# Norm outputs in chunks of 96 columns with ones behind each chunk: diagonal sums and plain sums from the same matmuls, in the backward pass of a spectral block with a gated MLP

## The chip, the cores and the metric

The kernel runs on one core of a Trainium2 chip. A core has five engines with queues of their own: TensorE (PE, with PEld for its weight loads), VectorE (DVE), ScalarE (ACT), GpSimd (POOL) and SyncE (SP, here used to issue DMAs). Engines run their instructions in order and wait for one another through semaphores. The metric is the device time of one execution, in microseconds (us).

## The reference

One block with two modulated norms, a global spectral filter (A) and a gated bilinear MLP (B), and then the gradients of the whole by its eight inputs. S = 2048 rows, D = 576 columns, F = 4608, everything in bfloat16.

```python
mod = (silu(c) @ w_mod)                     # six rows of 576: sa, ca, ga, sb, cb, gb
h = layernorm(x) * (1 + ca) + sa
x = x + ga * irfft2(rfft2(h) * (w_r + 1j * w_i))
h = layernorm(x) * (1 + cb) + sb
x = x + gb * ((h @ w_gate) * (h @ w_up)) @ w_down
out, vjp = jax.vjp(f, x, w_r, w_i, w_gate, w_up, w_down, c, w_mod)
grads = vjp(grad_out)
```

The change is about the gradients of the modulation rows. With gh the gradient at h (one row of 576 for each of the 2048 positions) and n the norm's output, the gradient of a shift row (sa, sb) is the plain sum of gh over the positions, and that of a scale row (ca, cb) is the sum of gh · n over the positions, column by column. ga's row is the sum of gx · y in the same way (gx the gradient, y the filter's output); gb's is made earlier.

## The kernel before

Positions are worked in 16 tiles of 128 (NT = 16), the columns of the MLP in blocks of 128 (NFB = 36). A forward part makes the two norms and the spectral filter, a long middle part (on PE nearly throughout) makes the gradients of the MLP, and a tail (from L811) makes the backward of the second norm, of the spectral filter and of the first norm. Into the tail's stages the MLP's last projection is woven, so that PE always has work.

What the change touches:

- **Norm outputs.** The stage of the first norm (L359 to L383) makes n1 on ACT (L372) from x, in groups of 4 tiles, uses it on DVE (nm, L374) and stores it to DRAM (n1_d, L378, on POOL). The stage of the second norm (L554 to L578) does the same for n2 in groups of 2 tiles (L570, L572, L575). The tiles come from pools that rotate two buffers.
- **Tail stage 1**, backward of the second norm: a pipeline of four steps over the 16 tiles (t1_norm L969, t1_turn L995, t1_cols, t1_rows). t1_norm loads n2's and y's tile, multiplies (gn) and calls norm_back (L868). t1_turn makes a transpose and adds the tile's part of the modulation sums into three PSUM banks csA, csB, csC.
- **Tail stage 2** (L1131 to L1178): the spectral filter's backward, untouched by the change.
- **Tail stage 3**, backward of the first norm: t3_rows L1194, t3_cols L1202 and t3_norm L1216 over 16 tiles, with the sums in csD and csE. t3_cols builds gh on DVE from two PSUM banks, one of them copied by ACT (ye, L1212; gh's halves L1213 and L1214). t3_norm makes gn (L1223) and calls norm_back, whose steps for the first norm are: ACT u with its row sum (L871), DVE product with its row sum (L873), DVE ab (L875), DVE u + residual (L876), ACT w (L878), DVE ob (L881). `ld3["last"]` is the last of these.
- **The sums.** PE has no sum of elementwise products, so `diag` (L910) multiplies gh (as weights) by n, 128 columns by 128 columns, over the positions; the wanted sums stand on the diagonal of each 128 x 128 product, and all tiles add up in the same bank. Four chunks of 128 columns and one of the last 64 make 576. `colsum` (L907) makes the plain sums: pick, a matrix of zeros with 64 columns of ones, as weights, and half of gh (288 columns) as the moving side, one matmul for each half, into rows 0 to 63 and 64 to 127 of one bank. The banks are opened and closed by matmuls of zeros (add_zero, L902).
- **Getting the sums out.** `diag_rows` (L917) masks the diagonals with the identity on DVE (dcb, dga, dca). The plain sums are copied (dsb L1043, dsa L1240). Each is spread to all 128 partitions by a matmul (`spread`, L924): of_rows (L930) with a matrix of ones, of_sums (L933) with sel, two masks that POOL fills at L1104.
- **Sections.** `section` (L936) takes one row of sums, copies the two spread halves into dmb on ACT (L939; dmb has two buffers), loads the slice of w_mod, multiplies on ACT (o8) and on DVE (pr, L952, five products with sums). Six sections hang on tiles of the last projection loop (L1264 to L1305): MSB at tile 8, MCB 9, MGA 10, MGB 11, MSA 12, MCA 13, each traced under an order constraint behind the tile's last matmul and behind ld3["last"].
- **What sets the order.** A scheduler orders each engine's instructions by priority and readiness in its own time. On PE `deal` (L883) writes the order of the tail's steps out by hand and deals a fixed number of projection matmuls into each step (16 a step in stage 1, 12 in stage 2, 20 and then 16 in stage 3); the spreads are not in that list and are placed by the scheduler.

Of the kernel before, what the change touches and what calls it, by code (L numbers as in the profile page):

```python
# [9 lines left out]
FP32 = mybir.dt.float32  # L10
# [9 lines left out]
NT = 16  # L20
S = 2048
D = 576
DP = 640
DF = 289
FP = 292
# [73 lines left out]
def build(ctx, tc, A_x, A_w_r, A_w_i, B_w_gate, B_w_up, B_w_down, c_in, w_mod, grad_out,  # L99
# [13 lines left out]
    def dram(name, shape, dt):  # L113
        return nc.dram_tensor(name, list(shape), dt).ap()
# [10 lines left out]
    wn_d = dram("wn_d", [128, 2 * NT * FP], BF)  # L125
    n1_d = dram("n1_d", [128, NT, D], BF)
    n2_d = dram("n2_d", [128, NT, D], BF)
    MSA, MCA, MGA, MSB, MCB, MGB = range(6)
# [12 lines left out]

    pick = glob.tile([128, 2, 128], BF, name="pick")
    nc.vector.memset(pick[:], 0.0)
    for q in range(2):
        nc.vector.memset(pick[:, q, 64 * q:64 * q + 64], 1.0)


    def traced():
# [111 lines left out]
    with ExitStack() as hs:  # L260
# [98 lines left out]
        def s1_norm(t):  # L359
            c4, tt = t // 4, t % 4  # L360
            if tt == 0:
                if c4 == 1:
                    with tc.issue_after(first):
                        x_load(3)
                n1s[c4] = hw2.tile([128, 4, D], BF, name="n1")
            if t == 0 or tt == (1 if c4 == 0 else 0):
                n = 1 if t == 0 else 4 - tt
                nmr = norm_stats(xts[c4][:, tt:tt + n, :], hw2, n, "ln1", rstd1g[:, t:t + n], 4)
                for k in range(n):
                    n1s["nmr", t + k] = nmr[:, k:k + 1]  # L370
# [3 lines left out]
            nc.vector.tensor_tensor(out=nm[:], in0=n1[:, tt, :], in1=modh[MCA][:], op=MUL)  # L374
# [157 lines left out]


        uts, ybs, h2_made = {}, {}, []

# [18 lines left out]
        def s3_norm(sa):  # L554
# [14 lines left out]
            for i in range(2):  # L569
                nc.scalar.activation(out=n2[:, i, :], in_=x1[:, i, :], func=ACT.Identity, bias=nmr2[:, i:i + 1], scale=rstd2g[:, s0 + i:s0 + i + 1])  # L570
                nm = hw2.tile([128, D], BF, name="nm")
                nc.vector.tensor_tensor(out=nm[:], in0=n2[:, i, :], in1=modh[MCB][:], op=MUL)  # L572
                nc.vector.tensor_tensor(out=h2p[:, s0 + i, D:DP], in0=nm[:, 512:D], in1=modh[MSB][:, 512:D], op=ADD)
                h2_made.append(nc.vector.tensor_tensor(out=h2p[:, s0 + i, 0:D], in0=nm[:], in1=modh[MSB][:], op=ADD).ins)
# [236 lines left out]
    with ExitStack() as ts:  # L811
# [56 lines left out]
        def norm_back(pool, gn, n, rstd, res, out, name):  # L868
# [6 lines left out]
            nc.vector.tensor_scalar(out=ab[:], in0=s12[:], scalar1=-1.0 / D, scalar2=None, op0=MUL)  # L875
            nc.vector.tensor_tensor(out=u[:], in0=u[:], in1=res, op=ADD)  # L876
            if name == "1":
                nc.scalar.activation(out=w[:], in_=n, func=ACT.Identity, bias=ab[:, 0:1], scale=ab[:, 1:2])  # L878
            else:
                nc.vector.tensor_scalar(out=w[:], in0=n, scalar1=ab[:, 1:2], scalar2=ab[:, 0:1], op0=MUL, op1=ADD)  # L880
            return nc.vector.tensor_tensor(out=out, in0=u[:], in1=w[:], op=ADD)  # L881
# [19 lines left out]

        def add_zero(*banks, first):  # L902

            for cs in banks:
                nc.tensor.matmul(cs[:], lhsT=ident[:], rhs=zero[:], start=first, stop=not first)

        def colsum(cs, h, src):  # L907
            nc.tensor.matmul(cs[:, 0:288], lhsT=pick[:, h, :], rhs=src, start=False, stop=False)

        def diag(cs, cs4, off, a, b):  # L910

            for m in range(5):
                o = cs[:, wide(m)] if m < 4 else cs4[:, off:off + 64]
                w = 128 if m < 4 else 64
                nc.tensor.matmul(o, lhsT=a[:, wide(m)] if m < 4 else a[:, D - 128:D], rhs=b[:, m * 128:m * 128 + w], start=False, stop=False)

        def diag_rows(pool, cs, cs4, off, name):  # L917

            d = pool.tile([128, D], FP32, name=name)
            nc.vector.tensor_tensor(out=d[:, 0:512].rearrange("p (m n) -> p m n", m=4), in0=cs[:].rearrange("p (m n) -> p m n", m=4), in1=ident[:].unsqueeze(1).to_broadcast([128, 4, 128]), op=MUL)  # L920
            nc.vector.tensor_tensor(out=d[:, 512:576], in0=cs4[:, off:off + 64], in1=ident[:, 64:128], op=MUL)
            return d
# [10 lines left out]
        def of_sums(d):  # L933
            return [lambda h=h: spread(sel[:, h, :], d[:]) for h in range(2)]

# [18 lines left out]
        with ExitStack() as r1:  # L954
# [14 lines left out]
            def t1_norm(t):  # L969
                if t == 0:  # L970
                    nc.sync.dma_start(ga_h[:], modb_d[:, MGA, :])
                for k, src, tt in [("n2c", n2_d, 0)] * (t == 0) + [("n2c", n2_d, t + 1)] * (t < NT - 1) + [("yc", y_d, t)]:
                    ld[k, tt] = c1.tile([128, D], BF, name=k, bufs=5 if k == "n2c" else 3)
# [21 lines left out]
            def t1_turn(t):  # L995
# [7 lines left out]
                if t == 0:  # L1003
                    add_zero(csA, csB, csC, first=True)
# [34 lines left out]
            in_order(seq)  # L1039
            dcb = diag_rows(tl, csA, csB, 288, "dcb")  # L1040
            dga = diag_rows(tl, csC, csB, 352, "dga")
            dsb = tl.tile([128, 288], FP32, name="dsb")
            nc.vector.tensor_copy(dsb[:], csB[:, 0:288])  # L1043
            with behind([i_ for i_ in nc.cur_bb.bb.instructions[-40:] if i_.engine == mybir.EngineType.DVE][-1:]):
# [57 lines left out]
        with behind([last[nc.gpsimd]]):  # L1102
            gb_h = modh(MGB, "gb_h", gbhp, nc.gpsimd)
            for q in range(2):  # L1104
                nc.gpsimd.tensor_copy(sel[:, q, :], ident[:, 64 * q:64 * q + 1].to_broadcast([128, 128]))
            nc.gpsimd.memset(ones_b[:], 1.0)
            nc.gpsimd.memset(gsc[:], 0.0)
# [108 lines left out]
        def t3_norm(sa):  # L1216
            for k, src in (("n1c", n1_d), ("gxc", gx1_d)):
                ld3[k] = c3.tile([128, D], BF, name=k, bufs=5)
                nc.sync.dma_start(ld3[k][:], src[:, sa, :])
# [7 lines left out]
            if sa == 0:  # L1227
                add_zero(csD, csE, first=True)
# [9 lines left out]
        dca = diag_rows(tl, csD, csE, 288, "dca")  # L1238
# [141 lines left out]
```

## Time and profile before

| | us |
|---|---|
| runs of the kernel, median of 3 (lowest to highest) | 1526.43 (1525.81 to 1529.65) |
| the profiled execution, its own time | 1524.87 |
| its span in the trace | 1523.1 |
| tail stage 1 | about 1260 to 1335 |
| tail stage 2 | about 1335 to 1390 |
| tail stage 3 | about 1390 to 1454 |
| the rest, projection and sections | 1454 to the end |

In the rows of a timeline the first number is the start in us from the span's start, the second the duration, then engine, line, operation, output and inputs, their sizes, and how many instructions in a row the entry holds; a bracket gives the idle time of the engine ahead of it and what ended that. In groups the last numbers are busy time and mean ns, then idle time before. A duration of one matmul holds the length of its pipeline; a stream of them overlaps. "clock" in a window's row is the granted TensorE clock as a share of full speed.

### The profile page before, as it was taken

How to read it: one execution, taken by the hardware profiler on the slowest of the kernel's cores; microseconds unless marked ns; L12 is line 12 of the kernel's file. 1: busy time of each engine (PE TensorE's matmuls, PEld its weight loads, DVE VectorE, ACT ScalarE, POOL GpSimd, SP SyncE). 2: the span in 40 equal slices, each digit the busy share in tenths (PEclk: the TensorE clock that was granted, in tenths of full speed). 3: DMA queues.
4: the chain of work that ended last, by engine and by line, in shares of the span. 5: the costliest groups of instructions: out<-in, count | busy, mean ns of one | idle time of the engine just before them, and what ended most of it. 6: DMA issues, size and time to landing. Idle time of an engine off the chain costs nothing. (4 is left out here: it accounts for less than half of the span.)

```text
span 1523.1 us, 29031 instructions
## 1 busy us (share of the span) xinstructions
PE 1490.3 (98%) x11140; PEld 1012.6 (66%) x11144; DVE 1060.6 (70%) x2646; ACT 583.4 (38%) x1189; POOL 238.8 (16%) x363
## 2 busy tenths in 40 slices
PE   6899999999999999999999999999999999999998
PEld 4666543566666667666666676676666667888876
DVE  6866753666677767667677677676676768688884
ACT  6667742322222222222222222222222225686763
POOL 0001222101101102111111120120110113221022
PEclk9999999999999999999999999999999999999999
DMA  8968999688878768768778588688677779965587
GB/s 317 282 200 224 278 255 249 152 162 155 174 129 161 155 125 174 152 125 177 135 146 178 118 159 164 119 163 156 137 152 153 132 175 252 305 220 181 182 290 201
DMA packets 487181, 280.42 MB, mean 184 GB/s; under 512 B 408865, under 2 KB 457378, under 8 KB 486018
## 3 DMA queue, kind: packets, MB, share of 16 engines
q1 hardware_dynamic: 458882, 175.32, 55.6%
q0 software_dynamic: 28160, 103.25, 23.0%
q8 instruction: 87, 1.43, 0.4%
q14 instruction: 52, 0.43, 0.1%
HBM read 108.62 MB, written 82.31 MB: 125 GB/s over the span
## 5 line engine op out<-in xcount | busy, mean ns | idle before, releaser
L752 DVE TENSOR_TENSOR acc<-acc,u8p 128x288 f32<-128x288 f32 (+1 forms) x1088 | 483.3, 453 | 276.1 <-PE u8p L747 272.6
L747 PE MATMUL u8p<-wT,ggT 128*128 128x288 bf16 x1152 | 328.0, 286 | 1.7 <-DVE acc L752 1.6
L747 PE MATMUL u8p<-wT,guT 128*128 128x288 bf16 x1152 | 327.6, 286 | 0.0
L711 PE MATMUL gup<-h2T,wgu 128*128 128x512 bf16 x1152 | 297.8, 379 | 0.0
L646 ACT CAST so<-u57p 128x288 bf16<-128x288 f32 x216 | 86.3, 400 | 532.8 <-PE u57p L644 522.1
L644 PE MATMUL u57p<-h2p,gu_sf 128*128 128x288 bf16 x1152 | 186.4, 286 | 0.0
L644 PE MATMUL u57p<-h2p,gg_sf 128*128 128x288 bf16 x1152 | 185.9, 286 | 0.0
L711 PEld LDWEIGHTS <-wgu 128*128 128x128 bf16 x1152 | 109.6, 98 | 97.9 <-issue 17.1
L747 PEld LDWEIGHTS <-ggT 128*128 128x128 bf16 x1152 | 112.6, 98 | 66.5 <-issue 14.0
L451 PE MATMUL u4p<-goT,wdT 128*128 128x512 bf16 x656 | 151.1, 379 | 0.9 <-DVE goT L423 0.5
L747 PEld LDWEIGHTS <-guT 128*128 128x128 bf16 x1152 | 112.7, 98 | 57.6 <-issue 2.4
L1286 PE MATMUL u3p<-wd,hl 128*128 128x288 bf16 x936 | 141.3, 288 | 0.1
L713 ACT CAST gT<-gup 128x512 bf16<-128x512 f32 x144 | 84.5, 587 | 131.5 <-PE gup L711 129.6
L644 PEld LDWEIGHTS <-hh_sf 128*128 128x128 bf16 x1152 | 112.7, 98 | 28.4
L644 PEld LDWEIGHTS <-gu_sf 128*128 128x128 bf16 x1152 | 112.4, 98 | 28.5
L644 PEld LDWEIGHTS <-gg_sf 128*128 128x128 bf16 x1152 | 112.4, 98 | 28.2
L1286 PEld LDWEIGHTS <-hl 128*128 128x128 bf16 x1152 | 107.8, 98 | 25.7 <-DMA hl<-hhT_d 0.4
L713 ACT CAST uT<-gup 128x512 bf16<-128x512 f32 x144 | 84.5, 587 | 77.4 <-PE gup L711 77.4
L451 PEld LDWEIGHTS <-wdT 128*128 128x128 bf16 x656 | 61.3, 98 | 73.0 <-issue 7.6
L644 PE MATMUL u57p<-gonC,hh_sf 128*128 128x288 bf16 x576 | 99.7, 286 | 0.0
L724 POOL DMA_DIRECT2D hhT_d<-hhT x36 | 33.3, 925 | 375.5 <-DVE hhT L715 352.5
L173 DVE CAST ghh_st<-u4p 128x512 bf16<-128x512 f32 x56 | 38.7, 691 | 59.0 <-PE u4p L451 58.9
(373 smaller groups left out, 1867.6 us busy)
## 6 DMA issues: line engine op xcount, KB each, us to landing
ghhT_d<-ghh_st POOLq DMA_DIRECT2D x36, 512.0 KB, 4.3
ghh<-ghhT_d POOLq DMA_DIRECT2D x36, 512.0 KB, 7.3
hhT_d<-hhT POOLq DMA_DIRECT2D x36, 512.0 KB, 6.4
hl<-hhT_d SPq DMA_DIRECT2D x28, 576.0 KB, 6.0
out_dram<-woT SPq DMA_DIRECT2D x70, 128.0 KB, 2.0
wdn<-in_B_w_down_dram SPq DMA_DIRECT2D x18, 288.0 KB, 3.6
wd<-in_B_w_down_dram POOLq DMA_DIRECT2D x36, 144.0 KB, 4.7
out_dram<-so SPq DMA_DIRECT2D x36, 144.0 KB, 2.8
```

The lines of the kernel that those rows point to most:

```text
L173: nc.vector.tensor_copy(dst, src)
L451: nc.tensor.matmul(pt[:], lhsT=wdTs[k][:, j, m, :], rhs=goT[:, 4 * sb4:4 * sb4 + 4, m, :], start=(m == 0 and n == 5), stop=(m == n - 1))
L644: mm = nc.tensor.matmul(pw[0][:, 0:288], lhsT=sf[:, t, :], rhs=rhs_n(t, h * 288, 288), start=(t == 0), stop=(t == NT - 1))
L646: followed(mm, nc.scalar.copy(so[:, h * 288:(h + 1) * 288], pw[0][:, 0:288]))
L711: nc.tensor.matmul(pts[k][:], lhsT=wgu[:, 4 * wi_ + m, jw * 128:(jw + 1) * 128], rhs=h2T[:, ts_, m, :], start=False, stop=(m == 3))
L713: nc.scalar.copy((gT, uT)[wi_][:, th_, :], pts[k][:])
L724: nc.gpsimd.dma_start(hhT_d[:, :, fb, :].rearrange("tp f x -> f tp x"), hhT[:].rearrange("f (tp ti) p -> f tp (ti p)", ti=2))
L747: nc.tensor.matmul(pu[:, 0:288], lhsT=l_, rhs=r_, start=(k == 0), stop=(k == len(mms) - 1))
L752: summed[t] = nc.vector.tensor_tensor(out=ghb(t)[:, hs_] if fbs[-1] == NFB - 1 else dst, in0=dst, in1=pu[:, 0:288], op=ADD).ins
L1286: mm = nc.tensor.matmul(p2[ti][:, 0:288], lhsT=hls[fb // 9][:, fb % 9, ti * 128:(ti + 1) * 128], rhs=w[:, fb - f0, h * 288:(h + 1) * 288], ...
```

## The change

n1 and n2 are stored as six chunks of 96 columns with two columns of ones behind each (DN = 6 × 98 = 588 columns for 576). Their tiles are two fixed buffers each, whose ones are written once by POOL. All operations on n go through a view (`part`) of six runs of 96; n1_d and n2_d and the tiles loaded from them have 588 columns.

`diag` works on six chunks of 96 columns. For gh · n the moving side of each matmul is 97 columns wide, 96 of n and one of ones, so that the last column holds the plain sums of gh; for gx · y it is 96 wide. The sixth chunk takes its weights from the last 128 columns. colsum, pick and the closing add_zero are gone: the last matmul into a bank closes it.

The plain sums are now a column of 128 values for each chunk: diag_sums copies six columns ([128, 6], two copies) where a row of [128, 288] was copied. of_sums multiplies the identity by each of these columns (three operations of DVE for a half, into one buffer dx of 288 columns) and spreads that with the matrix of ones. sel is gone, and a tile gap_l of 816 fp32 columns takes its place in the pool, so that the tiles behind keep their places.

```diff
-    pick = glob.tile([128, 2, 128], BF, name="pick")
...
+    def part(ap):
+        return ap.rearrange("p (m c) -> p m c", m=6)[:, :, 0:DC]
+    def ones_between(ap):
+        nc.gpsimd.memset(ap.rearrange("p t (m c) -> p (t m) c", c=DS)[:, :, DC:DS], 1.0)
...
+        n1r = [hw2.tile([128, 4, DN], BF, name="n1r%d" % k, bufs=1) for k in range(2)]
+        for n_ in n1r:
+            ones_between(n_[:])
...
-                n1s[c4] = hw2.tile([128, 4, D], BF, name="n1")
+                n1s[c4] = n1r[c4 % 2]
...
-            nc.scalar.activation(out=n1[:, tt, :], in_=xts[c4][:, tt, :], func=ACT.Identity, bias=n1s["nmr", t], scale=rstd1g[:, t:t + 1])
+            nc.scalar.activation(out=part(n1[:, tt, :]), in_=part(xts[c4][:, tt, :]), func=ACT.Identity, bias=n1s["nmr", t], scale=rstd1g[:, t:t + 1])
...
-            n2 = hw2.tile([128, 2, D], BF, name="n2")
+            n2 = n2r[sa // 2 % 2]
...
-        sel = tl.tile([128, 2, 128], FP32, name="sel")
+        tl.tile([128, 816], FP32, name="gap_l")
...
-            nc.vector.scalar_tensor_tensor(out=w[:], in0=gn[:], scalar=rstd, in1=n, op0=MUL, op1=MUL, accum_out=s12[:, 1:2])
+            nc.vector.scalar_tensor_tensor(out=part(w[:]), in0=part(gn[:]), scalar=rstd, in1=part(n), op0=MUL, op1=MUL, accum_out=s12[:, 1:2])
...
-                nc.scalar.activation(out=w[:], in_=n, func=ACT.Identity, bias=ab[:, 0:1], scale=ab[:, 1:2])
+                nc.scalar.activation(out=part(w[:]), in_=part(n), func=ACT.Identity, bias=ab[:, 0:1], scale=ab[:, 1:2])
...
-        def diag(cs, cs4, off, a, b):
-            for m in range(5):
-                o = cs[:, wide(m)] if m < 4 else cs4[:, off:off + 64]
-                w = 128 if m < 4 else 64
-                nc.tensor.matmul(o, lhsT=a[:, wide(m)] if m < 4 else a[:, D - 128:D], rhs=b[:, m * 128:m * 128 + w], start=False, stop=False)
+        def diag(cs, cs6, off, a, b, step, w, last_, shut=True):
+            for m in range(6):
+                o = cs[:, m * w:m * w + w] if m < 5 else cs6[:, off:off + w]
+                c0 = m * DC if m < 5 else D - 128
+                nc.tensor.matmul(o, lhsT=a[:, c0:c0 + 128], rhs=b[:, m * step:m * step + w], start=False, stop=last_ and m >= 4 and (m == 4 or shut))
+        def chunks(cs, cs6, off, w):
+            for m0, m1, mask, src in ((0, 5, ident[:, 0:DC], cs[:, 0:5 * w]), (5, 6, ident[:, 128 - DC:128], cs6[:, off:off + w])):
+                yield m0, m1, mask.unsqueeze(1).to_broadcast([128, m1 - m0, DC]), src.rearrange("p (m c) -> p m c", c=w)
...
+        def diag_sums(pool, cs, cs6, off, name):
+            d = pool.tile([128, 6], FP32, name=name)
+            for m0, m1, _, src in chunks(cs, cs6, off, DC + 1):
+                nc.vector.tensor_copy(d[:, m0:m1].unsqueeze(2), src[:, :, DC:DC + 1])
+            return d
...
         def of_sums(d):
-            return [lambda h=h: spread(sel[:, h, :], d[:]) for h in range(2)]
+            def half(h):
+                x = secp.tile([128, 288], FP32, name="dx", bufs=1)
+                for m in range(3 * h, 3 * h + 3):
+                    mask = ident[:, 0:DC] if m < 5 else ident[:, 128 - DC:128]
+                    nc.vector.tensor_scalar(out=x[:, m % 3 * DC:m % 3 * DC + DC], in0=mask, scalar1=d[:, m:m + 1], scalar2=None, op0=MUL)
+                return spread(ones_f[:], x[:])
+            return [lambda h=h: half(h) for h in range(2)]
...
-                for h in range(2):
-                    colsum(csB, h, gh[:, h * 288:(h + 1) * 288])
-                diag(csA, csB, 288, gh, n2c)
-                diag(csC, csB, 352, gx, yc)
-                if t == NT - 1:
-                    add_zero(csA, csB, csC, first=False)
+                diag(csA, csB, 0, gh, n2c, DS, DC + 1, t == NT - 1, False)
+                diag(csC, csB, 128, gx, yc, DC, DC, t == NT - 1)
...
-            dsb = tl.tile([128, 288], FP32, name="dsb")
-            nc.vector.tensor_copy(dsb[:], csB[:, 0:288])
+            dsb = diag_sums(tl, csA, csB, 0, "dsb")
...
-            for h in range(2):
-                colsum(csE, h, gh[:, h * 288:(h + 1) * 288])
-            diag(csD, csE, 288, gh, n1)
-            if sa == NT - 1:
-                add_zero(csD, csE, first=False)
+            diag(csD, csE, 0, gh, n1, DS, DC + 1, sa == NT - 1)
...
-        dsa = tl.tile([128, 288], FP32, name="dsa")
-        nc.vector.tensor_copy(dsa[:], csE[:, 0:288])
+        dsa = diag_sums(tl, csD, csE, 0, "dsa")
```

More of the change, by code (lines that the diff above doesn't have):

```diff
@@ L23 @@
 DP = 640
+DC = 96
+DS = 98
+DN = 6 * DS
 DF = 289
@@ L531, in build @@
         hw2 = pool("hc3", 2, "right")
+        n2r = [hw2.tile([128, 2, DN], BF, name="n2r%d" % k, bufs=1) for k in range(2)]
+        for n_ in n2r:
+            ones_between(n_[:])
         uts, ybs, h2_made = {}, {}, []
@@ L900, in wide, with add_zero @@
             return slice(m * 128, (m + 1) * 128)
-        def add_zero(*banks, first):
+        def add_zero(*banks):
             for cs in banks:
-                nc.tensor.matmul(cs[:], lhsT=ident[:], rhs=zero[:], start=first, stop=not first)
-        def colsum(cs, h, src):
-            nc.tensor.matmul(cs[:, 0:288], lhsT=pick[:, h, :], rhs=src, start=False, stop=False)
-        def diag(cs, cs4, off, a, b):
-            for m in range(5):
-                o = cs[:, wide(m)] if m < 4 else cs4[:, off:off + 64]
-                w = 128 if m < 4 else 64
-                nc.tensor.matmul(o, lhsT=a[:, wide(m)] if m < 4 else a[:, D - 128:D], rhs=b[:, m * 128:m * 128 + w], start=False, stop=False)
@@ L917, in diag_rows @@
-        def diag_rows(pool, cs, cs4, off, name):
-            d = pool.tile([128, D], FP32, name=name)
-            nc.vector.tensor_tensor(out=d[:, 0:512].rearrange("p (m n) -> p m n", m=4), in0=cs[:].rearrange("p (m n) -> p m n", m=4), in1=ident[:].unsqueeze(1).to_broadcast([128, 4, 128]), op=MUL)
-            nc.vector.tensor_tensor(out=d[:, 512:576], in0=cs4[:, off:off + 64], in1=ident[:, 64:128], op=MUL)
+                nc.tensor.matmul(cs[:], lhsT=ident[:], rhs=zero[:], start=True, stop=False)
@@ new lines, in diag_rows @@
+        def diag_rows(pool, cs, cs6, off, w, name):
+            d = pool.tile([128, D], FP32, name=name)
+            for m0, m1, mask, src in chunks(cs, cs6, off, w):
+                nc.vector.tensor_tensor(out=d[:, m0 * DC:m1 * DC].rearrange("p (m n) -> p m n", n=DC), in0=src[:, :, 0:DC], in1=mask, op=MUL)
+            return d
[3 more added lines that the diff above has]
+                nc.vector.tensor_copy(d[:, m0:m1].unsqueeze(2), src[:, :, DC:DC + 1])
@@ L972, in t1_norm @@
                 for k, src, tt in [("n2c", n2_d, 0)] * (t == 0) + [("n2c", n2_d, t + 1)] * (t < NT - 1) + [("yc", y_d, t)]:
-                    ld[k, tt] = c1.tile([128, D], BF, name=k, bufs=5 if k == "n2c" else 3)
+                    ld[k, tt] = c1.tile([128, DN if k == "n2c" else D], BF, name=k, bufs=5 if k == "n2c" else 3)
                     with behind(ld["order"]):
@@ L1003, in t1_turn @@
                 if t == 0:
-                    add_zero(csA, csB, csC, first=True)
-                for h in range(2):
-                    colsum(csB, h, gh[:, h * 288:(h + 1) * 288])
-                diag(csA, csB, 288, gh, n2c)
-                diag(csC, csB, 352, gx, yc)
-                if t == NT - 1:
-                    add_zero(csA, csB, csC, first=False)
+                    add_zero(csA, csB, csC)
+                diag(csA, csB, 0, gh, n2c, DS, DC + 1, t == NT - 1, False)
+                diag(csC, csB, 128, gx, yc, DC, DC, t == NT - 1)
             def t1_cols(t):
@@ L1039, in build @@
             in_order(seq)
-            dcb = diag_rows(tl, csA, csB, 288, "dcb")
-            dga = diag_rows(tl, csC, csB, 352, "dga")
-            dsb = tl.tile([128, 288], FP32, name="dsb")
-            nc.vector.tensor_copy(dsb[:], csB[:, 0:288])
+            dcb = diag_rows(tl, csA, csB, 0, DC + 1, "dcb")
+            dga = diag_rows(tl, csC, csB, 128, DC, "dga")
+            dsb = diag_sums(tl, csA, csB, 0, "dsb")
             with behind([i_ for i_ in nc.cur_bb.bb.instructions[-40:] if i_.engine == mybir.EngineType.DVE][-1:]):
@@ L1217, in t3_norm @@
             for k, src in (("n1c", n1_d), ("gxc", gx1_d)):
-                ld3[k] = c3.tile([128, D], BF, name=k, bufs=5)
+                ld3[k] = c3.tile([128, DN if k == "n1c" else D], BF, name=k, bufs=5)
                 nc.sync.dma_start(ld3[k][:], src[:, sa, :])
```

21 lines of the change are left out of this document (8 added, 13 removed).

## The prediction

> **What bounds the kernel now.** I read the page's busy shares first, then the windows around the changed code, then the timelines of TensorE (PE), VectorE (DVE) and ScalarE (ACT) there. The sum is made against the profiled execution (1524.87 us, span 1523.1); the runs' median is 1526.43, 1.56 above it, and I add that difference at the end. What a measurement of this kernel can tell from no change is about 0.3%, 4.6 us.
>
> ```profile
> PE 1490.3 (98%) x11140; PEld 1012.6 (66%) x11144; DVE 1060.6 (70%) x2646; ACT 583.4 (38%) x1189; POOL 238.8 (16%) x363
> ```
> ```profile
> 1260.00:1335.00 75.00, 73.65 (x722) 59.59 (x723) 52.25 (x150) 47.34 (x119) 22.59 (x38) 1.00 0.96 286
> ...
> 1390.00:1460.00 70.00, 69.61 (x620) 55.96 (x620) 56.80 (x150) 49.43 (x109) 5.49 (x11) 1.00 0.62 198
> ```
>
> PE is busy 98% of the whole and nearly all of both tail stages (columns: length, then busy time of PE, PEld, DVE, ACT, POOL, clock, DMA share, GB/s). So PE columns taken out of a stage shorten it, unless another engine's loop is equally long. That is asked stage by stage.
>
> **Tail stage 1 (second norm's backward, 1260 to 1335).** One tile's sums on PE:
>
> ```profile
> 1302.75 0.41 PE L908 MATMUL csB<-acc,pick 128*128 128x288 bf16 x2
> 1302.99 0.39 PE L915 MATMUL csA<-n2c,acc 128*128 128x128 bf16 x4
> 1303.22 0.19 PE L915 MATMUL csB<-n2c,acc 128*128 128x64 bf16 x1
> 1303.24 0.39 PE L915 MATMUL csC<-yc,gxr 128*128 128x128 bf16 x4
> 1303.47 0.19 PE L915 MATMUL csB<-yc,gxr 128*128 128x64 bf16 x1
> 1303.50 1.14 PE L1286 MATMUL u3p<-wd,hl 128*128 128x288 bf16 x8
> ```
>
> The first column is the start; a duration holds the pipeline's length too, so cost is start to start. The block runs from 1302.75 to 1303.50: 0.75. Two of 288 columns take 0.24, four of 128 take 0.23 (0.0575 each), one of 64 takes 0.02 to 0.03. After the change there are again 12 matmuls, six of 97 columns and six of 96: 1158 columns for 1728. No row has 96 or 97; halfway between 64 and 128 I take 0.0425 each, so 12 × 0.0425 = 0.51, a saving of 0.24 a tile and 16 × 0.24 = 3.8 in the stage. Bounds: if a short matmul costs what one of 128 does, 0.75 − 0.69 = 0.06 to 0.07 a tile, 1.1 in all; if it costs no more than 0.03, 0.39 a tile, 6.2 in all.
>
> The Trainium skill, "TensorE: Matmul & The Clock Gate" (section "Back-to-back issue gap"), says that a stream of weight load and matmul pairs of 128 columns holds about 81 ns each, against some 56 ns for one by itself, since the weight load sets the spacing too. The rows above show 57 ns for 128 columns, each with weights of its own, so the trace speaks against the larger figure; by it the change would save next to nothing here, because 12 matmuls stay 12.
>
> Does PE set the pace? The last tile's sums close with three matmuls of zeros, and then DVE reads them:
>
> ```profile
> 1329.40 0.38 PE L905 MATMUL csB<-zero,ident 128*128 128x512 bf16 x1
> 1329.61 0.38 PE L905 MATMUL csC<-zero,ident 128*128 128x512 bf16 x1
> ```
> ```profile
> 1329.60 0.69 DVE L920 TENSOR_TENSOR dcb<-csA,ident 128x512 f32<-128x512 f32 x1 [9.70 <-PE csB L915]
> ```
>
> DVE had been idle for 9.70 us when PE reached the end: PE is the slow one, and the whole 3.8 counts. The closing zeros go: three at a pitch of 0.21 (1329.40 to 1329.61) are 0.63, all on PE's path.
>
> **Tail stage 3 (first norm's backward, 1390 to 1454).** Here the sums of one tile are two of 288 and one set of five, 7 matmuls and 1152 columns; afterwards 6 and 582.
>
> ```profile
> 1405.94 0.41 PE L908 MATMUL csE<-ghr,pick 128*128 128x288 bf16 x2
> ...
> 1406.43 0.78 PE L1286 MATMUL u3p<-wd,hl 128*128 128x288 bf16 x5
> ```
>
> 0.49 becomes 6 × 0.0425 = 0.255: PE has 0.24 less in each step. But another loop is as long as PE's step:
>
> ```profile
> 1405.17 0.46 DVE L1213 TENSOR_TENSOR ghr<-yp,ye 128x289 bf16<-128x289 f32 x1
> ...
> 1406.02 0.46 DVE L1223 TENSOR_TENSOR gn<-ghr,opca_h 128x576 bf16<-128x576 bf16 x1
> ...
> 1408.55 0.46 DVE L881 TENSOR_TENSOR ob<-u,w 128x576 bf16<-128x576 bf16 x1 [0.58 <-ACT w L878]
> 1408.92 0.46 DVE L1213 TENSOR_TENSOR ghr<-yp,ye 128x289 bf16<-128x289 f32 x1
> ```
> ```profile
> 1406.51 0.78 ACT L871 ACTIVATE u<-gn,rstd1g 128x576 bf16<-128x576 bf16 x1 [0.48 <-DVE gn L1223]
> ...
> 1407.65 0.87 ACT L878 ACTIVATE w<-n1c,ab 128x576 bf16<-128x576 bf16 x1 [0.27 <-DVE ab L875]
> ```
>
> L1213 of one tile to L1213 of the next is 3.75, and in between each link waits for the one before: gn, ACT's u with its sum, DVE's ab, ACT's w, DVE's ob after 0.58 idle, then at once the next L1213, which waits for no PE. Nothing in this chain becomes shorter, so PE's 0.24 turns into PE's idle time, 15 times. Only one step has DVE waiting for data that PE's work holds up:
>
> ```profile
> 1396.82 0.46 DVE L1213 TENSOR_TENSOR ghr<-yp,ye 128x289 bf16<-128x289 f32 x1 [0.73 <-ACT ye L1212]
> ```
>
> There 0.24 is gained once. The two closing zeros (2 × 0.21 = 0.42) stand behind the last tile's work and end in PE's slack too; I count nothing for them.
>
> **The end.** The gradients of the six modulation rows are spread on PE and multiplied on DVE and ACT in sections. PE meets them in its own order and waits:
>
> ```profile
> 1475.64 1.19 PE L927 MATMUL spp<-dgb,ones_f 128*128 128x288 f32 x2 [2.40 <-ACT dmb L939]
> 1476.62 5.85 PE L1286 MATMUL u3p<-wd,hl 128*128 128x288 bf16 x36
> 1482.31 4.57 PE L1286 MATMUL u3q<-wd,hl 128*128 128x288 bf16 x36
> ```
> ```profile
> 1475.00:1480.00 5.00, 4.36 (x20) 2.80 (x21) 4.03 (x13) 4.73 (x9) 0.00 (x0) 0.66 0.71 227
> ```
>
> The buffer of dmb is free only when DVE has finished the MSB section's products, which stand behind DVE's backlog from stage 3's end. So DVE's work between 1454 and 1475 is on the path. The change adds six small operations there (three of 96 columns for each half of MSB) and takes the long copy of dsa away.
>
> ```profile
> L1127 DVE SCALAR_TENSOR_TENSOR gwt<-Xn,b_Vp 128x64 f32<-128x64 bf16 x4 | 0.6, 223 | 0.0
> ...
> L1043 DVE COPY dsb<-csB 128x288 f32<-128x288 f32 x1 | 0.4, 449 | 0.0
> ```
>
> A row of 64 columns is listed at 0.22; DVE rows overlap by 0.09 (ob above: 0.46 long, 0.37 to the next), so six at about 0.15 are 0.9, less 0.36 for the copy: +0.55. I take +0.5; bounds 0 (another hole of DVE's takes them up) and +1.1 (0.18 each, and the two tiny copies that replace the long one cost as much). PE's wait of 2.40 becomes about 2.9. The second half of MSB needs the one dx buffer back from the first half's spread, which PE does as it meets it; that risk is the slower rival. The same six for MSA come after DVE's backlog has cleared: taken as 0.
>
> After this wait the granted clock is 0.66 in the window and 36 projection matmuls take 5.69 start to start (1476.62 to 1482.31), against 4.41 for the next 36 by their duration less the same overlap (4.57 − 0.16). The cost of 1.3 is in the time of before already and stays. The Trainium skill, same page (section "HAM oscillation — how this bites in real kernels"), sets the danger line at gaps of more than about 3.4 us; in this trace a gap of 2.40 was followed by the lower clock, so the row decides, and by neither would 0.5 us more change the sum.
>
> **What I cost at nothing.** Chunked operands: the same ACT cast of 292 columns costs the same contiguous and scattered in fours:
>
> ```profile
> L1018 ACT CAST zt<-zp 128x292 bf16<-128x292 f32 x32 | 12.3, 407 | 4.4 <-PE zp L1017 4.3
> ...
> L1026 ACT CAST b_Vp<-vp 128x292 bf16<-128x292 f32 x32 | 11.3, 405 | 6.3 <-PE vp L1025 6.3
> ```
>
> So runs of 96 should be free on ACT (bounds 0 to +0.1 an operation, for DVE too, where no row compares). The 2% longer rows of n1 and n2 and the four memsets of ones lie in the forward stages beside PE; POOL, which does the memsets, is busy 16%. The removed pick and sel were written under PE's work, so nothing comes back for them. POOL's last load of down weights in stage 1 is triggered by work of that stage and takes 8.4 to land:
>
> ```profile
> wd<-in_B_w_down_dram POOLq DMA_DIRECT2D x1, 1152.0 KB, 8.4
> ```
>
> PE comes to its first use earlier by what it has gained by then, but the trigger, itself paced by PE's stage, comes earlier too: 0, at most +1, the share of the 3.8 gained in the 4 or 5 steps that 8.4 cover (5 × 0.24 = 1.2, one of them before the trigger).
>
> **Sum.** −3.8 − 0.63 − 0.24 + 0.5 = −4.2: profiled 1520.7, median **1522.2**. Own range ±1.5.
>
> **Rivals.**
>
> *Stage 3 gains too* (1518.2). The instruction order is a scheduler's; if in its new order L1213 of the next tile comes into the hole of 0.58 ahead of ob, the loop is 3.75 − 0.58 = 3.17, shorter than PE's 3.75 − 0.24 = 3.51, and PE paces again: 15 × 0.24 = 3.6 and 0.42 more, together −8.2. For it: the hole is there in every step. Against: the same instructions stand on DVE as before, so nothing asks for another order.
>
> *Short matmuls are no cheaper than those of 128* (1525.0). Then −1.1 − 0.63 − 0.15 (one step of stage 3: 0.49 − 6 × 0.0575) + 0.5 = −1.4. For it: five in a row take 0.25 in both sets, which 0.05 each would give as well as a price by columns; the one of 64 is never followed by another short one. Against: the 64 itself passes in 0.02 to 0.03.
>
> *PE waits at the new masks* (slower, 1532.8). PE runs its instructions in order, and MSB's spread stands early:
>
> ```profile
> 1450.32 1.44 PE L927 MATMUL spp<-dsb,sel 128*128 128x288 f32 x4
> ```
> ```profile
> 1454.45 0.46 DVE L881 TENSOR_TENSOR ob<-u,w 128x576 bf16<-128x576 bf16 x1
> ```
> ```profile
> 1485.56 0.76 DVE L952 SCALAR_TENSOR_TENSOR pr<-wmj,dmb 128x576 bf16<-128x576 bf16 x1 [0.78 <-DMA wmj<-in_w_mod_dram]
> ```
>
> Before, it needed only dsb, ready since stage 1. Now its right side is DVE's dx, which has to stand behind the last L881. If PE keeps its place in the order, it waits 1454.83 + 0.3 − 1450.3 = 4.8. MSA's second half can stall alike behind five products at up to 0.76 and the wait of 0.78: up to 4.4. A lowered clock adds 1.8 (1.3, and half of the spread's 0.98 from 1475.64 to 1476.62): 11.0; less the gains of 4.7, +6.3. It is slower than before as soon as these waits exceed 4.7. Against: the scheduler places the spread by when its input is ready, so it should move it behind other matmuls.
>
> *Chunked views cost in stage 3's loop* (1525.4). If the two operations with n1 in the chain (L873 is beside ACT's u, L878 is in the chain) take 0.1 each more, the loop is 0.2 longer, 16 × 0.2 = 3.2, and −4.2 + 3.2 leaves −1.0: the change would not do what its columns promise. The ACT rows speak against it.
>
> **How the numbers follow.** Forecast 0.45; stage 3 gains 0.22; no cheaper than 128: 0.15; waits at the masks 0.12; chunked views 0.06. Faster by over 0.3% means below 1521.85: two fifths of the forecast (0.18) and nearly all of the first rival (0.21), 0.39. Slower by over 0.3% (above 1531.0) takes 9.3 of waits: 0.09, of which 0.08 from the masks. Within: 0.52. The range: below, the stage 3 case less a little, 1517.6; above, both no-gain cases with the bounds of the load and of the masks (+1 and +1.1 on 1525.4), 1527.5. It leaves out most of the slower case and the edge of the stage 3 case, under 0.2.
>
> **What would show it.** Stage 1: the block ahead of L1286 takes 0.51 in place of 0.75, DVE's wait ahead of dcb shrinks by about 4 and stays above 4, no zeros before it. Stage 3: L1213 to L1213 stays 3.75 and PE shows idle time of about 0.24 a step; the first rival shows 3.5 and PE without gaps, the chunked views 3.9 and longer L878 rows. The end: a wait of about 2.9 ahead of dgb's second half; the slower rival shows a PE wait of several us ahead of a spread of dx. I am wrong if the block stays near 0.7, or if spreads wait together for more than 5.

## The result and the profile after

The changed kernel takes 1524.88 us in the median of 20 runs (1517.52 to 1533.90); the kernel before takes 1530.11 in 20 runs beside them (1524.14 to 1537.85). The ratio is 0.9963, 95% interval 0.9946 to 0.9981: about 5.6 us faster, between 2.9 and 8.2. In a second set of runs it was 0.9955 (0.9932 to 0.9978). The forecast was 4.2 us less. As a time it was 1522.2, against 1526.43 for the kernel before; that kernel measured 3.7 more in these runs, so the differences are what to compare.

The profiled execution took 1528.38 (span 1526.6), longer than the profiled one of before, although the kernel is faster in the median. Both pages have to be read stage by stage to see why. The page after:

```profile
span 1526.6 us, 29006 instructions
...
PE 1486.6 (97%) x11121; PEld 1006.7 (66%) x11123; DVE 1060.8 (69%) x2657; ACT 582.8 (38%) x1189; POOL 238.8 (16%) x365
```

PE's busy time fell by 3.7, but its share fell too: new idle time has appeared. The first piece of it has nothing to do with the change's matmuls. In the timeline of PE after:

```profile
206.93 1.24 PE L459 MATMUL u4p<-goT,wdT 128*128 128x512 bf16 x5 [2.98 <-DVE ghh_st L178]
```

Here, at the end of the forward part, DVE was late, having waited 4.00 for a tile of x to land, and PE waited for DVE. The part from the first matmul into u4p to the first into gup, most of the forward part, took 255.8 in this execution, 248.7 in the profiled one before, and between 248.3 and 257.6 in 13 profiles, with no order by kernel (before, two of them with an edit described below: 248.7, 250.5, 256.7, 250.4; changed: 255.8, 250.5, 249.9). In the kernel before this is most of the scatter between the profiles, whose spans go from 1523.1 to 1528.2. So from here on I compare stages, not spans.

**Stage 1's sums** after, in the timeline of PE:

```profile
1290.01 0.39 PE L923 MATMUL csA<-n2c,acc 128*128 128x97 bf16 x5
1290.24 0.21 PE L923 MATMUL csB<-n2c,acc 128*128 128x97 bf16 x1
1290.28 0.37 PE L923 MATMUL csC<-yc,gxr 128*128 128x96 bf16 x5
1290.49 0.21 PE L923 MATMUL csB<-yc,gxr 128*128 128x96 bf16 x1
1290.53 1.14 PE L655 MATMUL u57p<-h2p,gu_sf 128*128 128x288 bf16 x8
```

From 1290.01 to 1290.53 is 0.52, where it was 0.75. Yet the stage did not become shorter in this execution, for later in it stands:

```profile
1314.91 0.56 PE L923 MATMUL csC<-yc,gxr 128*128 128x96 bf16 x5 [3.34 <-DMA yc<-y_d]
```

PE waited 3.34 for a tile of y, and from 1314.4 on the granted clock was 0.5 for 3.4 us. I call such a stretch a half-clock window.

**Stage 3** after, first DVE, then PE:

```profile
1412.07 0.45 DVE L1233 TENSOR_TENSOR ghr<-yp,ye 128x289 bf16<-128x289 f32 x1
...
1415.83 0.46 DVE L1233 TENSOR_TENSOR ghr<-yp,ye 128x289 bf16<-128x289 f32 x1
```
```profile
1415.11 0.60 PE L215 MATMUL upa<-T_GB,j_A 128*128 128x256 bf16 x4
1415.76 0.27 PE L217 MATMUL upb<-T_GB,j_At 128*128 128x128 bf16 x2
1415.87 0.90 PE L1301 MATMUL u3p<-wd,hl 128*128 128x288 bf16 x6
1416.60 0.40 PE L923 MATMUL csD<-n1c,ghr 128*128 128x97 bf16 x5
```

DVE's step is 3.76 as before. PE's slack shows between upa and upb: 0.65 from start to start, where four matmuls of 256 columns take 0.44 when nothing holds them (before, and in the fuller steps of an experiment below).

**The end** after, where PE had waited 2.40 ahead of the second half of dgb:

```profile
1466.11 0.75 PE L947 MATMUL spp<-dx,ones_f 128*128 128x288 f32 x2 [0.49 <-DVE dx L958]
...
1473.04 0.75 PE L947 MATMUL spp<-dga,ones_f 128*128 128x288 f32 x2 [0.49 <-ACT dmb L966]
...
1480.98 1.13 PE L947 MATMUL spp<-dgb,ones_f 128*128 128x288 f32 x4
```

dgb's two halves now run together without a wait. MSB's spreads, which the scheduler had put among stage 3's last steps, now come after 51 projection matmuls, 4 and 5.5 us behind the last tile's ob, and PE waits 0.49 for the masks. The change therefore did something at the end that I had not counted, and stage 1 did less than I had counted. The experiments are about these two.

### The profile page after: what moved, and what is told of

Read it like the earlier page. It is cut to its first block, busy times and chain, and to the rows that moved or that the text cites. A ratio compares the mean times of both kernels' runs of the same rounds, so it can differ in the third digit from the quotient of the medians.

```text
span 1526.6 us, 29006 instructions
## 1 busy us (share of the span) xinstructions
PE 1486.6 (97%) x11121; PEld 1006.7 (66%) x11123; DVE 1060.8 (69%) x2657; ACT 582.8 (38%) x1189; POOL 238.8 (16%) x365
## 4 chain that ended last, share of the span: by engine, by line
PE 84%; DMA 5%; DVE 4%; issue 3%; ACT 2%; POOL 0%; SPq 0%; POOLq 0%; DVEq 0%; ACTq 0%
PE u57p L655 27%; PE u8p L758 18%; PE gup L722 17%; PE u4p L459 8%; PE u3p L1301 4%; PE gup L717 3%; DMA yc<-y_d 1%; DMA wmj<-in_w_mod_dram 1%; PE zp L398 1%; DMA xc<-in_A_x_dram 1%; DMA wdT<-wdn 1%; DVE ln_st L186 1%; PE u3q L1301 1%; PE u4p L454 1%; PE zp L1040 1%
```

## The experiments

Each profiled kernel gives the same few lengths, which tell more than the times: stage 1 from the first to the last matmul with yc; the end from stage 3's first matmul (upa) to the last projection matmul (u3p or u3q). In us, one profile each:

| kernel | stage 1 | trigger of the wd load after stage 1's start | upa to last projection | last projection to the end |
|---|---|---|---|---|
| before | 66.92 | 40.2 | 127.30 | 7.8 |
| before_again | 66.91 | 40.7 | 127.09 | 7.8 |
| before_split | 66.90 | 39.9 | 127.09 | 6.3 |
| before_q18 | 66.91 | 39.8 | 125.24 | 9.5 |
| changed | 68.46 | 43.0 | 124.38 | 7.2 |
| after_again | 66.31 | 41.7 | 125.20 | 6.9 |
| after_pair | 63.75 | 38.9 | 125.27 | 6.7 |
| after_q18 | 66.11 | 41.5 | 126.21 | 5.6 |
| after_early | 65.09 | 41.5 | 124.92 | 6.4 |
| after_split | 63.59 | 39.2 | 124.56 | 6.1 |
| split_pair | 67.66 | 44.1 | 125.33 | 6.4 |
| after_all | 64.82 | 40.1 | 122.92 | 5.6 |
| all_pair | 71.99 | 46.3 | 123.03 | 5.6 |

### Both kernels once more (before_again, after_again)

> The kernel before, unchanged, for a second profile. Theory A (the waits that I read are the program's own): the wait ahead of the second spread of dgb is again 2 to 3 us, with a half-clock window behind it, stage 1 takes 66.9 us from the first to the last matmul with yc, and PE has no wait over 1 us between 200 and 1260. Theory B (they are chance of one execution's transfers): the wait for dmb differs by over 1 us or is gone, and other waits of several us stand elsewhere.

> The changed kernel, unchanged, for a second profile. Theory A: the wait of 3.3 us for yc in stage 1 and that of 3.0 us for ghh_st near 207 us, each followed by a half-clock window, come from the change and are seen again. Theory B (chance of late transfers): both are gone or stand elsewhere, stage 1 takes 66.9 less 3.5 = 63.4 us from the first to the last matmul with yc, and the step of stage 3 is 3.76 us.

The waits of PE from stage 3 on, before_again and then after_again (columns: total, times, longest):

```profile
PE spp L927 <- ACT dmb L939: 2.4, 1, 2.4
PE u3p L1286 <- DMA hl<-hhT_d: 1.6, 1, 1.6
```
```profile
PE spp L947 <- DVE dx L958: 1.2, 2, 0.7
PE upb L217 <- ACT ye L1232: 1.2, 2, 0.8
PE csD L923 <- DVE ghr L1233: 0.7, 1, 0.7
PE spp L947 <- ACT dmb L966: 0.5, 1, 0.5
```

The end of before is the program's own: the wait of 2.4 for dmb is there again (and 2.5 in before_split), and in after_again it is 0.5 again. The half-clock window behind that wait is not the program's own: the same 2.4 left the clock at full speed in before_again, as its windows say (the 1.00 ahead of the DMA share), and PE then ran into a wait of 1.6 for hl instead. Nor was it free of waits over 1 us between 200 and 1260, as expected: there are 1.07 at 206.84 and 1.26 at 1257.74.

```profile
1460.00:1480.00 20.00, 17.64 (x136) 13.63 (x135) 16.40 (x43) 10.64 (x19) 3.22 (x5) 1.00 1.00 361
```

In stage 1 neither theory was right as it stood. The wait for yc is gone in after_again, but not the loss: the stage takes 66.31 and not 63.4, and PE waits elsewhere. The chain of after_again shows for what (start, length, what):

```profile
1291.65 12.24 DMA wo_l<-so
1304.62 8.36 DMA wd<-in_B_w_down_dram
```

The load of down weights starts only when a transposing DMA of the tile so into wo_l has landed, and PE waits for the load. That the load takes the place of the tile so is my reading of the program; that it is released by this DMA is in the trace, where POOL's wait ahead of the load includes the semaphore of that DMA and ends with it. The issues on SP and POOL of after_again:

```profile
1291.65 1.65 SPq L667 DMA_TRANSPOSE wo_l<-so  x1
...
1303.91 0.40 SPq L674 DMA_DIRECT2D out_dram<-wo_l  x1
```
```profile
1304.62 0.90 POOL L1086 DMA_DIRECT2D wd<-in_B_w_down_dram  x1 [5.75 <-DMA n2c<-n_d]
```
```profile
1313.03 1.14 PE L1301 MATMUL u3p<-wd,hl 128*128 128x288 bf16 x8 [2.33 <-DMA wd<-in_B_w_down_dram]
```

In all 13 profiles POOL issues the load 0.7 us after SP issues the store of wo_l, that is, when the transposing DMA has landed (the releaser in the bracket is inferred, and is another transfer). Before the change the load was issued 39.8 to 40.7 after stage 1's start, and PE came to its first use at 49.7 (1311.98 in the profiled execution before): enough. In after_again PE came there at 47.7 (1313.03 less the wait of 2.33), and the load, issued at 41.7 and 8.4 on its way, landed at 50.0.

### 18 projection matmuls a step in stage 3 (after_q18, before_q18)

```diff
-                q = 16 if stage == 1 else 12 if stage == 2 else 20 if k == 0 else 16
+                q = 16 if stage == 1 else 12 if stage == 2 else 20 if k == 0 else 18
...
-  ... tag="cs" + "AB"[n3 // 2 % 2]) if tp_ > 4 and n3 % 2 else ...
+  ... tag="cs" + "AB"[n3 // 2 % 2]) if tp_ > 5 and n3 % 2 else ...
...
-                proj += pe_since(mark) if tp_ < 5 else []
+                proj += pe_since(mark) if tp_ < 6 else []
```

> The changed kernel with 18 instead of 16 projection matmuls dealt into each step of stage 3 (and the sixth pair of tiles taken into the dealt list, with its banks from the pool of the earlier ones). Theory 1 (stage 3 is held by the loop of DVE and ACT, PE has 0.24 us a step to spare): two matmuls of 0.122 fit in, the step stays at 3.76 and 36 matmuls fewer stand behind stage 3, so 4.4 us less after it and about 4 us less in all than the changed kernel, 0.990 to 0.995 of the kernel before. Theory 2 (PE still paces stage 3): the step grows to 4.0 and the time is that of the changed kernel, 0.996.

> The kernel before with the same 18 projection matmuls a step in stage 3. Theory 1: before the change PE's step equals the DVE and ACT loop, both 3.76, so the step grows to 4.0, stage 3 by 4.2, the part behind it shrinks by 4.4: ratio 0.999 to 1.001. If it comes out at 0.997 or less, PE had room before the change too, and theory 1 is wrong on what the change freed.

The sums of two tiles in a row, after_q18 and then before_q18:

```profile
1427.44 0.39 PE L923 MATMUL csD<-n1c,ghr 128*128 128x97 bf16 x5
...
1431.22 0.39 PE L923 MATMUL csD<-n1c,ghr 128*128 128x97 bf16 x5
```
```profile
1428.45 0.41 PE L908 MATMUL csE<-ghr,pick 128*128 128x288 bf16 x2
...
1432.46 0.41 PE L908 MATMUL csE<-ghr,pick 128*128 128x288 bf16 x2
```

The step is 3.78 in the changed kernel and 4.01 in the one before. Two matmuls of 0.122 fit into the one without cost and lengthen the other by their own time. So theory 1 holds: the change freed 0.24 a step on PE, and DVE and ACT hold the stage. The times: before_q18 1.0002 (0.9977 to 1.0026) as expected, after_q18 0.9963 (0.9940 to 0.9987), no better than the changed kernel. Where the 4 us went that theory 1 promised on top stands at the end, in its timeline of PE:

```profile
1487.00 0.72 PE L947 MATMUL spp<-dx,ones_f 128*128 128x288 f32 x2 [3.75 <-DVE dx L958]
```

PE is sooner at MSA's second spread, but DVE makes its masks where it made them before, among the products of an earlier section. This is the slower rival's mechanism, at the place that it named second. A half-clock window of 3.4 us (1.7 us lost) follows it.

### The load in two halves (after_split, split_pair, before_split)

```diff
-        queued_load(10, wd_load, 28, 8)
+        queued_load(10, wd_load, 28, 4)
+        queued_load(10, wd_load, 32, 4)
```

> The changed kernel with the last load of down weights in stage 1 (blocks 28 to 35) issued as two loads of four blocks. Theory W (what stage 1 gained on PE was given back to this load, which is released by a transfer that PE does not pace and takes 8.4 us to land): the first half lands about 4 us sooner, the wait of 2.3 us ahead of u3p falls to 0.5 or less (the second half is wanted 2 us after the first), stage 1 from the first to the last matmul with yc takes 63.9 to 64.6 us in place of 66.3, and the whole is about 2 us faster than the changed kernel, ratio near 0.995. Theory V (the wait is one execution's chance): the wait stands or falls without regard to the split and the ratio stays at 0.9963.

> The kernel before with the same split, as a control. Theory W: the load had come 1.1 us before its use there, so no wait goes and stage 1 stays at 66.9 us from the first to the last matmul with yc.

> The changed kernel with the load of blocks 28 to 35 in two halves, once more. Theory W: stage 1 takes 63.6 to 65 us and at least 1 us less than in the unsplit kernel beside it, with a wait for the load of 1 us at most. Theory V (chance): no shorter than the unsplit one. Ratio 0.993 to 0.997, in which 2 us against the unsplit kernel cannot be told apart by the time alone.

> The changed kernel once more, beside the next two on one chip. Theory W: stage 1 (first to last matmul with yc) is again held by a load of stage 1 and takes 65 to 66.5 us, not the 63.4 that its shorter steps add up to; from stage 3's first matmul to the last projection matmul 124.4 to 125.2 us against 127.1 before. Ratio 0.994 to 0.998.

after_split took 63.59 in stage 1, which is the full 3.3 less, and before_split 66.90, as expected. That looked like proof, and the repetition took it back: split_pair took 67.66, with the load triggered at 44.1, and the unsplit after_pair beside it 63.75, with the trigger at 38.9 and no wait in the stage. The SP and POOL rows of after_pair:

```profile
1291.41 1.48 SPq L667 DMA_TRANSPOSE wo_l<-so  x1
...
1300.50 0.39 SPq L674 DMA_DIRECT2D out_dram<-wo_l  x1
```
```profile
1301.21 0.90 POOL L1086 DMA_DIRECT2D wd<-in_B_w_down_dram  x1 [2.95 <-ACT zt L1041]
```

Here the transposing DMA landed 9.1 after its issue (1291.41 to 1300.50), in after_again 12.3. So the expectation for after_pair, that the stage would again be held by a load, failed too. Stage 1's length follows the trigger: up to 40.1 it takes 63.6 to 64.8, at 41.5 to 41.7 it takes 65.1 to 66.3, from 43.0 on 67.7 to 72.0. In the kernels before it never came later than 40.7.

But the trigger is only a sign of how late the transfers of this stretch land; the load is not all that PE waits for. In the profiled execution of the changed kernel and in all_pair PE had no wait for the load, and waited 3.34 and 5.53 for yc instead. Two DMA issues of that stretch in the changed kernel (1296 to 1302, the last number is the time to landing):

```profile
yc<-y_d SPq DMA_DIRECT2D x1, 144.0 KB, 15.2
...
wo_l<-so SPq DMA_TRANSPOSE x1, 13.5
```

This yc was issued 31.3 after the stage's start, as in after_pair, where it took 9.0 to land; in all_pair it was issued at 32.1 and took 16.6. With the waits for yc and for the load taken off, and half of the half-clock time behind them, stage 1 is 63.6 to 64.0 in all nine profiles of the changed kernel and its variants. So PE's saving is there each time, and what differs is the waits for these two transfers.

Theory W therefore holds in a wider form: transfers that PE does not pace decide the stage, the load in some executions and yc in others. Splitting the load does not mend it. Its first half landed after 5.0 to 7.5, where the whole took 7.3 to 9.1 in the changed kernels; the expectation had been about 4 sooner, and the trigger moves by more than is saved. The ratios of the two split runs, 0.9978 (0.9954 to 1.0002) and 0.9961 (0.9937 to 0.9986), do not tell the split kernel from the changed one.

The windows from the stage's first to its last matmul with yc, for before_again, after_again and after_pair (columns as in the prediction), show how near the edge it is:

```profile
1263.40:1330.30 66.90, 65.66 (x659) 53.52 (x657) 46.13 (x134) 43.48 (x109) 19.32 (x33) 1.00 0.96 279
```
```profile
1263.00:1329.30 66.30, 62.57 (x660) 50.92 (x658) 46.30 (x135) 43.29 (x109) 18.96 (x31) 1.00 0.99 277
```
```profile
1262.30:1326.10 63.80, 62.47 (x662) 50.93 (x660) 46.43 (x135) 43.36 (x110) 18.95 (x31) 1.00 1.00 288
```

PE's work in the stage fell by 3.1 to 3.2 in the two executions of the changed kernel, but the DMA engines' share was 0.96 before and is now 0.99 to 1.00: nearly the same bytes are asked for in less time, and there is nothing left. That this is why transfers land later is argued and not shown: no run took transfers out of the stage, and the share alone does not tell after_again from after_pair, which had 1.00 and no wait. Why one execution's transfers land later than another's stays open.

### MSB's masks early (after_early)

```diff
-        tl.tile([128, 816], FP32, name="gap_l")
+        tl.tile([128, 240], FP32, name="gap_l")
+        dxb = tl.tile([128, D], FP32, name="dxb")
...
             dsb = diag_sums(tl, csA, csB, 0, "dsb")
+            for m in range(6):
+                mask = ident[:, 0:DC] if m < 5 else ident[:, 128 - DC:128]
+                nc.vector.tensor_scalar(out=dxb[:, m * DC:m * DC + DC], in0=mask, scalar1=dsb[:, m:m + 1], scalar2=None, op0=MUL)
...
-        late = {8: (MSB, of_sums(dsb)), ...
+        late = {8: (MSB, of_rows(dxb)), ...
```

> The changed kernel with the six masked products for MSB made right behind stage 1, into a buffer of their own (in the place of the gap), so that MSB's two spreads need nothing of DVE at stage 3's end. Theory H (at the end the masks fill a hole of 3.1 us in which DVE waited for Xn, so they cost DVE nothing; PE pays only its waits of 0.5 to 0.7 in front of the spreads): the spreads go back to stage 3's last steps, PE's two waits for dx of MSB (0.5 to 1.2 us together) go, the wait for Xn comes back by about 1 us, the products of MSB start no more than 0.5 us sooner, and the time changes by less than 1 us. Theory P (my prediction: six masks lengthen DVE's chain by 0.9): the products start 0.9 us sooner and the last matmul comes 1 to 1.5 us sooner.

DVE's rows at the one filter gradient that waits for its transfer, in before_again, the changed kernel and after_early:

```profile
1466.62 1.29 DVE L1124 SCALAR_TENSOR_TENSOR gwt<-Xn,b_Vp 128x512 f32<-128x512 bf16 x2 [3.08 <-DMA Xn<-xn_d]
```
```profile
1472.68 1.29 DVE L1144 SCALAR_TENSOR_TENSOR gwt<-Xn,b_Vp 128x512 f32<-128x512 bf16 x2 [0.19 <-DMA Xn<-xn_d]
```
```profile
1463.29 1.29 DVE L1148 SCALAR_TENSOR_TENSOR gwt<-Xn,b_Vp 128x512 f32<-128x512 bf16 x2 [1.71 <-DMA Xn<-xn_d]
```

Theory H holds: the masks lie in a hole of 3.1 us in which DVE waited for Xn. Taken away, the wait is back by 1.5, and the products of MSB start at 82.1 after upa (81.3 to 81.9 in the changed kernel, 83.2 before): no sooner than with the masks. PE waits 1.64 for dmb, where the changed kernel has 0.5 for dmb and 0.5 to 1.2 for dx, and the last projection matmul comes at 124.92, as in the changed kernel (124.38 to 125.27). Theory H's last point, a time within 1 us of the changed kernel's, is not borne out by the ratio, 0.9998 (0.9975 to 1.0021) against 0.9963 (0.9946 to 0.9981). The intervals overlap, and nothing in the stages of its profile explains the difference; I do not read a cause into it.

### All three edits (after_all, all_pair)

> The changed kernel with all three edits: the split load, MSB's masks early, and 18 projection matmuls a step in stage 3. If stage 3 has room for two matmuls and only the late masks took that gain back (a wait of 3.7 us for dx), the step stays at 3.76, the last projection matmul comes 2 (load) + 4.4 (moved matmuls) us sooner than in the changed kernel, and the whole 3 to 6 us sooner: ratio 0.992 to 0.995. If the end is set by the last stores and not by PE, the last matmul comes sooner by as much but the time does not: 0.996.

> The three edits together once more (split load, MSB's masks early, 18 projection matmuls a step in stage 3). From stage 3's first matmul to the last projection matmul 122.9 us as in its first profile, 1.5 to 2.3 us less than the changed kernel, and stage 1 as in the split kernel. Ratio 0.992 to 0.996, below both others.

With the masks early and 18 matmuls a step the last projection matmul comes 122.92 and 123.03 after upa, 2 us sooner than in the changed kernel, in both profiles. It is 2 and not 4.4 because DVE's sections are now what PE waits for (2.2 for dmb and 1.7 for dx in all_pair). Stage 1 stayed what it is, 64.82 and 71.99. The times were 0.9947 (0.9924 to 0.9970) and 0.9912 (0.9882 to 0.9942, six runs against twelve of the others on that chip, where the changed kernel had 0.9955). It is the fastest of the kernels by the median both times, but its intervals overlap the changed kernel's, so that it is faster than the changed kernel is likely and not shown by the times. The expectation of 6.4 us sooner at the last matmul failed: the load's part of it was not there, and of the 4.4 for the moved matmuls 2 were.

## Why the prediction was right, and where not

The time was right, but by luck: two errors of the sum cancel. In means over three profiles each (before, before_again and before_split, whose edit leaves stage 1 and stage 3 as they were; the changed kernel, after_again and after_pair):

| term | predicted | measured |
|---|---|---|
| stage 1's sums (with the first tile's, 0.22) | −3.8 | −1.0 (66.91 to 66.17, and 0.22) |
| stage 1's closing zeros | −0.63 | −0.63 (last yc to last apt: 56.54 to 55.91) |
| stage 3 and the end | −0.24 + 0.5 | −2.2 (127.16 to 124.95) |
| last projection matmul to the end | 0 | −0.4 (7.3 to 6.9; −0.9 without before_split) |
| sum | −4.2 | −4.2 |

That the two sums agree to a tenth is chance as well: the mean of stage 1 rests on three executions between 63.75 and 68.46.

**Price of a short matmul: right.** 0.52 a tile for the 0.51 forecast, steps shorter by 0.225 to 0.235. The rival by which they cost as much as those of 128 is out: five of 97 take 0.23 and five of 96 take 0.21. The Trainium skill ("TensorE: Matmul & The Clock Gate", section "Back-to-back issue gap") gives a sustained figure of 81 ns for weight load and matmul at 128 columns. The trace before has 57 ns there, and the trace after has 42 to 46 ns at 96 and 97 columns, each matmul with its own weights; no run here shows the larger figure.

**"PE sets the pace, and the whole 3.8 counts": wrong.** I took DVE's idle 9.70 as proof that PE was the slow one, and it was, against DVE (which still waits 7.2 there). I did not hold the transfers against the shorter stage: yc has no term at all, and the load's was put at nothing. The step that failed is the sentence on the load of down weights: "the trigger, itself paced by PE's stage, comes earlier too: 0, at most +1". The trigger waits for a transposing DMA, and the load's slack before the change was about 1 us (40.2 + 8.4 against 49.7). In the three executions of the changed kernel PE waited 3.34 for yc, 2.33 for the load, and for neither. So the −3.8 became −1.0 in the mean, with single executions from −3.4 to +1.3.

**Stage 3 held by DVE and ACT: right.** The step stayed at 3.76, and the pair with 18 matmuls shows the slack. From upa to the last sum it is 64.56 before and 64.29 after in the mean: −0.28 for the −0.24. The rival in which the next L1213 moves ahead of ob did not occur, nor did the chunked views cost anything in that chain, which is as long as before.

**The end: wrong sign.** "+0.5" was DVE's added work taken as if DVE were busy all the time. The bound of 0 named the hole that takes it up, and the hole is in the trace of before, 3.1 us long, 10 us ahead of the wait that I did quote. Beyond that, the scheduler put the last tile's projection sums (of) ahead of ob, so the filter gradients start right behind ob, the next Xn is asked for 0.4 to 0.9 sooner, and the products of MSB end 1.3 to 2.0 sooner after upa (85.2 to 85.9 for 87.2). The wait for dmb fell from 2.4 to 0.5, and the new waits for masks are 0.5 to 1.2. The 1.3 of lowered clock behind that wait, which I said would stay, did not: none of the three changed executions has a half-clock window at the end, and two of the three before have one.

**The slower rival: right in kind, small in size.** The scheduler moved MSB's spreads, as "against" said, and PE waited 0.5 to 1.2 for masks in all. As soon as PE came sooner (after_q18), MSA's second half cost 3.75.

## What to carry to other kernels

Idle time of another compute engine shows who is slow among the engines, not that nothing else is near; before PE's saving is counted in full, each transfer that lands inside the stage has to be checked for its slack and for what releases its issue. A load that is released by another transfer need not come sooner when the engines do: the trigger here came 39.8 to 40.7 after the stage's start before the change, and 38.9 to 46.3 after it. And added work on an engine is priced by where its next hole is, not by its duration.

## What the runs showed of the hardware

The same wait of 2.4 to 2.5 us on PE was followed by a half-clock window of 3.4 us in two of three profiles of the kernel before (before, before_split) and by full clock in the third. At the wait of 5.5 for yc in all_pair the clock was at half for 6.8 us, and after_again's wait of 2.3 cost no clock. The Trainium skill ("TensorE: Matmul & The Clock Gate", section "HAM oscillation — how this bites in real kernels") sets the line at about 3.4 us of idle time. Here a gap of 2.4 may or may not cost the clock, so I price it as 0 to 1.7 us, half of a window of 3.4.

The transposing DMA ahead of the load, issued 28.5 to 31.8 us after stage 1's start, landed 7.3 to 9.9 us later in the four profiles of the kernels before and 9.1 to 17.0 us later in the nine of the changed ones. Stage 1 was 66.9 in all four of the former and varied from 63.6 to 72.0 in the latter.
